# RWKV attention and SwiGLU on one core: two more units turned by VectorE, weight sums on VectorE, last store in halves

## The chip, the cores and the metric

The kernel runs on one core of a Trainium2 chip. The metric is device time in microseconds, the median over several executions; one more execution was profiled.

## What is computed

The reference is an RWKV attention block and a SwiGLU feed-forward block behind it, all in float32:

```python
# r, k, v: (4 batches, 8 heads, 768 positions, 48); w, u: (8, 48)
for t in range(S):
    cur = einsum('bhd,bhe->bhde', u[None] * kt, vt)
    y[:, :, t] = einsum('bhd,bhde->bhe', rt, state + cur)
    state = w[None, :, :, None] * state + einsum('bhd,bhe->bhde', kt, vt)
x = y.transpose(0, 2, 1, 3).reshape(3072, 384)
g = x @ w_gate                      # 384 x 1536
out = (g * sigmoid(g) * (x @ w_val)) @ w_out   # 1536 x 384
```

## The kernel before

The sequence is cut into chunks of 128 positions. A chunk of one batch with all its heads is a **unit**; there are 24 units, numbered chunk by chunk, so that unit i is chunk i // 4 of batch i % 4. For each unit:

- `load` and `load_v` bring k, r and v in through SyncE's DMA queue. From unit 4 on, k and r land in two alternating buffers (`k_ld`, `r_ld`).
- `scale` (GpSimd, L299 and L302) multiplies k and r by powers of the decay and writes them to `hats`, a tile that holds four k buffers (`khat`) and two r buffers (`rhat`). Which r buffer a unit takes is told by `rhat_of`: units below `BLOCKS` alternate, later ones go by pairs.
- `own_product` (GpSimd, L228 and L229) and `own_sum` (VectorE, L234) form the term of the current position. `load(i)` overwrites what the `own_product` of unit i - 2 reads, and so waits for it.
- k and r must be turned, so that the head's dimension lies on the partitions. Units below `BLOCKS` (12 before) use `turn`: eight transposes on TensorE into PSUM (L341) and two copies by ScalarE (L345). Units from `BLOCKS` on use `move_blocks` and `turn_blocks`: sixteen DMAs from SyncE's queue (L356) move the 32x32 blocks of `hats` to their turned places in two more buffers (`blocks`, one set only), and VectorE then turns each block in place with two instructions (L371).
- `scores` (TensorE L379, VectorE L384), `outputs` (TensorE L409, ScalarE L413) and `update` (TensorE L424, VectorE L436, GpSimd L437) give the attention's output x, and the state for the next chunk.

Two units make a group g of 256 rows for the feed-forward block. The groups 0 and 1 use `gate_value` (six matmuls into a PSUM bank of the tag gv, a sigmoid on ScalarE, L455 and L456 on VectorE). Later groups go in pairs through `four` and `w_sums` (L585 to L641), and all pairs go through `project` (L519 to L542), which needs fewer products than the plain form because it adds and subtracts quarters of the operands first. For that, `weight_sum` (L476, GpSimd before) makes four differences of quarters of `wo`, once; `h_sums` (L492 to L496, VectorE) makes those of the hidden layer. `project(g, 0)` takes PSUM banks of the tag gv, which has two buffers.

The weights come in as bits of another format and are rounded on the way (L173 to L216) by ScalarE, VectorE and GpSimd, up to about step 9. `EARLY` says at which points of the steps 4 to 11 a piece of rounding or, once that is done, a `weight_sum` ("R") and a piece of the feed-forward work ("F") is put in.

The order on every engine is the order of the code, as each engine works through its own queue. In step s of the main loop (s = 4 to 25) come: `own_sum(s)`, `scale(s + 1)`, `own_product(s + 1)`, `load_v(s + 1)`, `load(s + 3)`, then `turn(s)`, then `scores(s - 1)`, `turn_blocks(s)`, `move_blocks(s + 1)`, and, in steps before 12, `outputs(s - 2)` and `update(s - 2)` late in the step (from step 12 on right behind `scores`). The pieces of the feed-forward work stand between them.

Of the kernel before, what the change touches and what calls it, by code (L numbers as in the profile page):

```python
# [15 lines left out]
P = 128  # L16
# [6 lines left out]
def fast(  # L23
# [31 lines left out]
    N = B * NCH  # L55
    DM, DFF = moe_w_gate.shape
# [11 lines left out]
    dve, pool, act, pe, sp = nc.vector, nc.gpsimd, nc.scalar, nc.tensor, nc.sync  # L68
# [26 lines left out]
    khat, rhat = [hats[:, n] for n in (0, 2, 3, 5)], [hats[:, n] for n in (1, 4)]  # L95
# [4 lines left out]
    blocks = [hats[:, n].rearrange("p h x -> p (h x)") for n in (7, 6)]  # L100

    def rhat_of(i):
        return rhat[i % 2 if i < BLOCKS else i % 4 // 2]

    def raw(i):

# [4 lines left out]
    def load(i):  # L111
        c, b = divmod(i, B)
        rows = slice(P * c, P * (c + 1))
        for src, dst in zip((k, r), raw(i)):
            sp.dma_start(out=dst, in_=src[b, :, rows, :].rearrange("h t d -> t h d"))

    def load_v(i):
        c, b = divmod(i, B)
        rows = slice(P * c, P * (c + 1))
        for e in range(2):  # L120
            sp.dma_start(
                out=v_ld[i % 4][:, :, 64 * e : 64 * e + D],
                in_=v[b, :, rows, :].rearrange("(a e) t d -> e t a d", e=2)[e],
            )
# [3 lines left out]
    for f in range(FC // 2):  # L128
        for src, dst in ((moe_w_gate, wg), (moe_w_val, wv)):
            cols = slice(2 * P * f, 2 * P * (f + 1))  # L130
# [94 lines left out]
    def own_product(i):  # L225
        kl, rl = raw(i)
        rk = two.tile([P, H, D], FP32, name="rk", tag="rk")[:]
        pool.tensor_mul(rk, rl, kl)  # L228
        pool.tensor_mul(rk, rk, ub[:])  # L229
        rks[i] = rk  # L230

    def own_sum(i):
        dus[i] = three.tile([P, H], FP32, name="du", tag="du")
        dve.tensor_reduce(dus[i][:], rks.pop(i), axis=AX.X, op=ALU.add)  # L234
# [9 lines left out]
    for e in range(2):  # L244
# [3 lines left out]
        out=ub[:].rearrange("p h d -> p (h d)"),  # L248
        in_=bass.AP(tensor=u.tensor, offset=u.offset, ap=[[0, P], [1, H * D]]),
# [9 lines left out]
    def warm(n):  # L259
# [9 lines left out]
        out=mask[:], in_=mask[:], compare_op=ALU.is_gt, fill=0.0,  # L269
# [7 lines left out]
    for l in range(7):  # L277
        n = 1 << l
# [15 lines left out]
    def at(i, a):  # L294

        return HP - 1 - a if i >= BLOCKS and i % 2 == 0 else a

# [3 lines left out]
    def scale_r(i):  # L301
        pool.tensor_mul(rhat_of(i)[:, :, 0:D], raw(i)[1], rscale[:])  # L302
# [8 lines left out]
    def scale(i):  # L311
        scale_k(i)
        scale_r(i)
# [18 lines left out]
    def pair(t, a):  # L332
        return t[:, 2 * a : 2 * a + 2, :].rearrange("p e d -> p (e d)")

    def turn(i):
        kr = khat[i % 4], rhat_of(i)
        tps = [ps_a.tile([P, HP, P], FP32, name="tp", tag="a") for _ in kr]
        turned[i] = three.tile([P, HP, P], FP32, name="rT", tag="rT")
        for tp, t, dst, table in zip(tps, kr, (kT[i % 2], turned[i]), (pw[:, :, 1 : P + 1], pv)):
            for a in range(HP):  # L340
                pe.transpose(tp[:, a, :], pair(t, a), ident[:])  # L341
            if i < 4:
                dve.tensor_mul(dst[:], tp[:], table)
            else:
                act.copy(dst[:], tp[:])  # L345
# [27 lines left out]
    def scores(i):  # L373

        ps = [ps_a.tile([P, HP, P], FP32, name="s_ps", tag="a") for _ in range(2)]
        for a in range(HP):
            for e in range(2):
                rows = slice(64 * e, 64 * e + D)
                pe.matmul(  # L379
                    ps[e][:, a, :], kT[i % 2][rows, at(i, a), :], turned[i][rows, at(i, a), :],  # L380
                    start=True, stop=True, skip_group_check=True,
                )
        for e in range(2):
            dve.copy_predicated(  # L384
                At[i % 2][:].rearrange("p (a e) t -> p a e t", e=2)[:, :, e],
                mask[:].bitcast(INT32).unsqueeze(1).to_broadcast([P, HP, P]), ps[e][:],
            )
# [77 lines left out]
    FH, NH = FC // 2, DM // 2  # L465
# [5 lines left out]
    def weight_sum():  # L471

        n = len(summed)
        o = (wt[1][:], w12, wt[0][:], wt[2][:])[n]
        a, b = ((w22, w12), (w12, w11), (w22, w12), (w21, wt[0][:]))[n]
        pool.tensor_sub(o, a, b)  # L476
        summed.append(n)

    part_of = {}
# [1 line left out]
    def h_quarters(g):  # L481
        return [
            hT[g][:, FH * k : FH * (k + 1), P * j : P * (j + 1)] for j in range(2) for k in range(2)
        ]
# [13 lines left out]
    def project(g, n):  # L498

        h11, h12, h21, h22 = h_quarters(g)  # L500
        x = part_of.setdefault(g, {})
        if n == 0:
            one_bank = ps_f.tile([P, 2, 2 * P], FP32, name="o_f", tag="gv")[:, 0, 0:NH]
            if g % 2 == 0:
                x["a"] = ps_o.tile([P, 2 * P], FP32, name="o_a", tag="o")[:, 0:NH]
                x["b"] = one_bank
            else:
                x["a"] = one_bank
                x["b"] = ps_w.tile([P, 2 * P], FP32, name="o_b", tag="w_mag")[:, 0:NH]
            x["out"] = [two.tile([P, DM], FP32, name=n, tag=n) for n in ("o_sb1", "o_sb2")]  # L510
        lhs, rhs, acc = (
            (h11, w11, "a"), (h12, w21, "b"), (1, wt[0], "a"), (2, wt[1], "a"),
            (0, w12, "b"), (h22, wt[2], "a"), (3, w22, "b"),
        )[n]
        if isinstance(lhs, int):
            lhs = x["s"][lhs]
        ps = x[acc]
        for f in range(FH):
            pe.matmul(  # L519
                ps, lhs[:, f, :], rhs[:, f, :],  # L520
                start=(f == 0 and n in (0, 1, 4)), stop=(f == FH - 1), skip_group_check=True,
            )
        o1, o2 = x["out"]
        if n in (0, 2, 3):
            nm = {0: "p1", 2: "u2", 3: "u3"}[n]
            x[nm] = six.tile([P, 2 * P], FP32, name=nm, tag="part")[:, 0:NH]
            act.copy(x[nm], ps)
        elif n == 1:
            dve.tensor_add(o1[:, 0:NH], x["p1"], ps)
        elif n == 5:  # L530
            act.copy(o2[:, 0:NH], ps)
        elif n == 6:
            dve.tensor_add(o1[:, NH:DM], x["u2"], ps)  # L533
        if n in (3, 4):
            if "c22" in x:
                dve.tensor_add(o2[:, NH:DM], x["u3"], x["b"])
            x["c22"] = True
        if n >= 5:
            j = 6 - n
            c, b = divmod(2 * g + j, B)  # L540
            n0 = S * b + P * c
            act.dma_start(out=out[n0 : n0 + P, :], in_=x["out"][j][:])  # L542

# [155 lines left out]
    def gaps(s, n):  # L701

        if s not in EARLY:
            if n == 0:
                share[0] = min(-(-len(todo) // (4 - (s - 9) % 4)), 14)
            feed(share[0] // 5 + (n < share[0] % 5))
            return
        for what in EARLY[s][n]:
            if what == "R":
                if done["pool"] < NW:  # L710
                    round_weights()
                elif len(summed) < 4:
                    weight_sum()
            else:
                feed(1, 3)

    share = [0]
    BLOCKS = 12
    LATE = 12
    EARLY = {s: ("" if s < 7 else "R", "F", "R", "F", "RF") for s in range(5, 12)}  # L720
    EARLY[4] = ("R", "F", "", "F", "F")
# [82 lines left out]
    for s in range(4, N + 2):  # L804
        if 4 < s < N:
            own_sum(s)
        if s + 1 < N:
            scale(s + 1)
            own_product(s + 1)
            load_v(s + 1)  # L810
            if s + 3 < N:
                load(s + 3)
        if s < BLOCKS:
            turn(s)
        gaps(s, 0)
        if 4 <= s - 1 < N:
            while small:
                small.popleft()()
            scores(s - 1)
            if s >= LATE:  # L820
                outputs(s - 2)
                update(s - 2)
            gaps(s, 1)
        if BLOCKS <= s < N:
            turn_blocks(s)
        if BLOCKS <= s + 1 < N:
            move_blocks(s + 1)
        gaps(s, 2)
        if s - 2 >= 4 and (s < LATE or s > N):
            outputs(s - 2)  # L830
            update(s - 2)
        if s >= 5 and s % 2:
            queue((s - 3) // 2)
        if s < N:
            diagonal(s)
        if s - 2 >= 4:
            gaps(s, 3)
        gaps(s, 4)
        if s == 12:

            dve.tensor_tensor(bad[:], held[:], wcol[:], ALU.not_equal)
            dve.tensor_reduce(badc[:], bad[:], axis=AX.X, op=ALU.add)
            dve.memset(ones[:], 1.0)
            n_ps = ps_a.tile([P, HP, P], FP32, name="n_ps", tag="a")
            pe.matmul(n_ps[0:1, 0, 0:1], badc[:], ones[:], start=True, stop=True)
            act.copy(outside, n_ps[0:1, 0, 0:1])
# [417 lines left out]
```

## Time and profile before

| | us |
|---|---|
| median of 6 runs (625.54 to 627.76) | 626.11 |
| the profiled execution, its own time | 625.23 |
| span of its profile | 623.4 |
| TensorE busy in the span | 611.2 |
| VectorE / ScalarE / GpSimd busy | 357.6 / 238.8 / 296.8 |

Times in the profile run from the start of the span. A line of a timeline gives the start, the time from the start of the first to the end of the last instruction of the row, the engine (PE TensorE, PEld its weight loads, DVE VectorE, ACT ScalarE, POOL GpSimd, SP SyncE; a q behind it is the engine's queue, for DMA issues), the line, the operation, what it writes and reads, how many instructions, and in brackets the idle time ahead of it with what ended it. Busy time of an engine that others do not wait for costs nothing.

### The profile page before, as it was taken

Reading aid. Unit: us, or ns where it says so; the run is one execution under the profiler, and the core shown is the slowest. Engines: PE = TensorE matmul, PEld = TensorE weight load, DVE = VectorE, ACT = ScalarE, POOL = GpSimd, SP = SyncE. Lnnn points to the kernel's source line nnn. Section 1 sums busy time; section 2 is a strip of 40 time slices with the busy share of each in tenths; the row PEclk is TensorE's granted clock in tenths of the full one; section 3 lists DMA queues with packets and bytes.
Section 4 is the critical chain, followed back from the end, with each engine's and each line's share of the span. In section 5 each row is a group of like instructions: output and inputs, shape, how many; then the busy total and the mean of one; then the engine's idle time right before and its main releaser. Section 6 shows DMA issues by size and latency. Waiting matters only on the chain.

```text
span 623.4 us, 13014 instructions
## 1 busy us (share of the span) xinstructions
PE 611.2 (98%) x5040; PEld 551.4 (88%) x5040; DVE 357.6 (57%) x751; ACT 238.8 (38%) x647; POOL 296.8 (48%) x350
## 2 busy tenths in 40 slices
PE   8899999999999999999999999999999999999996
PEld 7688888899888899888899888899988899988896
DVE  5888897373566574466575455574354463355460
ACT  3368795312444412344331335422244321333310
POOL 4789789935556315364452636341334211443110
PEclk9999999999999999999999999999999999999999
DMA  7989873233232213323223311221000000000001
GB/s 179 221 218 249 257 249 64 51 63 83 56 60 34 39 16 77 64 42 46 45 34 68 78 17 31 32 41 38 26 1 2 2 0 26 26 1 2 1 2 56
DMA packets 138008, 40.47 MB, mean 65 GB/s; under 512 B 128592, under 2 KB 131792, under 8 KB 137936
## 3 DMA queue, kind: packets, MB, share of 16 engines
q1 hardware_dynamic: 134480, 34.82, 26.3%
q10 hardware_dynamic: 3456, 4.72, 2.1%
q8 instruction: 42, 0.69, 0.5%
q14 instruction: 30, 0.25, 0.1%
HBM read 28.51 MB, written 4.72 MB: 53 GB/s over the span
## 4 chain that ended last, share of the span: by engine, by line
PE 90%; POOL 2%; DMA 1%; ACT 1%; DVE 1%; issue 0%; SPq 0%; ACTq 0%; POOLq 0%
PE c_b L625 25%; PE c_a L625 21%; PE o_f L519 13%; PE o_a L519 8%; PE gv L448 7%; PE o_b L519 6%; PE y_ps L409 5%; PE s_ps L379 3%; PE u_ps L424 1%; DMA r_ld<-in_r_dram 1%; PE tp L341 1%; POOL wg L216 1%; POOL wv L216 1%; POOL rk L228 0%; POOL hats L299 0%
## 5 line engine op out<-in xcount | busy, mean ns | idle before, releaser
L609 POOL TENSOR_TENSOR hT<-hT,u 128x256 f32<-128x256 f32 x60 | 47.1, 785 | 148.3 <-DVE hT L608 121.2
L632 ACT COPY u<-c_a 128x256 f32<-128x256 f32 x120 | 44.5, 371 | 86.1 <-PE c_a L625 83.3
L625 PE MATMUL c_a<-t,wv 128*128 128x256 f32 x240 | 72.0, 382 | 0.1
L625 PE MATMUL c_b<-xT,wg 128*128 128x256 f32 x240 | 71.6, 380 | 0.0
L605 ACT ACTIVATE sg<-hT 128x256 f32<-128x256 f32 x120 | 50.0, 416 | 52.4 <-DVE hT L634 33.8
L320 ACT ACTIVATE At<-ident,du 128x128 f32<-128x128 f32 x176 | 62.1, 400 | 15.5 <-DVE o_sb L533 7.2
L625 PE MATMUL c_b<-xT,s 128*128 128x256 f32 x240 | 61.6, 379 | 0.0
L639 DVE TENSOR_TENSOR u<-u,c_b 128x256 f32<-128x256 f32 x60 | 25.1, 419 | 60.5 <-PE c_b L625 53.7
L625 PEld LDWEIGHTS c_b<-xT,s 128*128 128x128 f32 x240 | 45.2, 190 | 6.6
L625 PEld LDWEIGHTS c_a<-t,wv 128*128 128x128 f32 x240 | 44.9, 190 | 6.9 <-ACT u L632 1.2
L625 PEld LDWEIGHTS c_b<-xT,wg 128*128 128x128 f32 x240 | 45.3, 190 | 6.0
L634 DVE TENSOR_TENSOR hT<-p,c_b 128x256 f32<-128x256 f32 x60 | 25.2, 420 | 42.0 <-PE c_b L625 39.4
L585 POOL TENSOR_TENSOR s<-wv,wg 128x256 f32<-128x256 f32 x24 | 17.8, 741 | 65.5 <-PE o_f L519 50.8
L384 DVE COPY_PREDICATED At<-mask,s_ps 128x512 f32<-128x512 int32 x48 | 33.1, 744 | 21.8 <-PE s_ps L379 12.8
L302 POOL TENSOR_TENSOR hats<-r_ld,rscale 128x384 f32<-128x384 f32 x20 | 20.8, 1039 | 35.2 <-DMA hats<-hats 24.6
L448 PE MATMUL gv<-xT,wg 128*128 128x256 f32 x144 | 36.7, 391 | 0.6 <-ACT xT L413 0.6
L637 DVE TENSOR_TENSOR hT<-hT,c_a 128x256 f32<-128x256 f32 x60 | 25.3, 421 | 19.4 <-PE c_a L625 18.1
L641 DVE TENSOR_TENSOR hT<-u,c_b 128x256 f32<-128x256 f32 x60 | 25.2, 420 | 19.4 <-PE c_b L625 19.2
L409 PE MATMUL y_ps<-At,v_ld 128*32 128x128 f32 x768 | 34.9, 273 | 1.4 <-DVE At L384 1.4
L625 PE MATMUL c_b<-t,s 128*128 128x256 f32 x120 | 36.2, 383 | 0.0
L625 PE MATMUL c_b<-xT,wv 128*128 128x256 f32 x120 | 35.9, 381 | 0.0
L625 PE MATMUL c_a<-t,s 128*128 128x256 f32 x120 | 35.8, 380 | 0.0
(135 smaller groups left out, 1382.8 us busy)
## 6 DMA issues: line engine op xcount, KB each, us to landing
hats<-hats SPq DMA_DIRECT2D x192, 32.0 KB, 2.0
w_bits<-in_moe_w_gate_dram SPq DMA_DIRECT2D x6, 768.0 KB, 6.5
v_ld<-in_v_dram SPq DMA_DIRECT2D x48, 96.0 KB, 3.2
w_bits<-in_moe_w_val_dram SPq DMA_DIRECT2D x6, 768.0 KB, 6.1
w_bits<-in_moe_w_out_dram SPq DMA_DIRECT2D x6, 768.0 KB, 6.8
out_dram<-o_sb ACTq DMA_DIRECT2D x24, 192.0 KB, 1.9
k_ld<-in_k_dram SPq DMA_DIRECT2D x20, 192.0 KB, 3.1
r_ld<-in_r_dram SPq DMA_DIRECT2D x20, 192.0 KB, 3.9
```

The source lines that it names most:

```text
L320: lambda h=h: act.activation(At[i % 2][:, h, :], ident[:], AF.Identity, scale=du[:, h : h + 1])
L384: dve.copy_predicated(At[i % 2][:].rearrange("p (a e) t -> p a e t", e=2)[:, :, e], mask[:].bitcast(INT32).unsqueeze(1).to_broadcast([P, H ...
L409: pe.matmul(ps[32 * q : 32 * q + 32, cc, :], *x, start=start, stop=stop, skip_group_check=True,)
L448: pe.matmul(gv[:, o, :].rearrange("p (i t) -> p i t", i=2), wt[:, c, P * f : P * (f + 1)], xT[:, 2 * g % NX : 2 * g % NX + 2, c, :], start ...
L519: pe.matmul(ps, lhs[:, f, :], rhs[:, f, :], start=(f == 0 and n in (0, 1, 4)), stop=(f == FH - 1), skip_group_check=True,)
L605: act.activation(x[what, f][:], h[j], AF.Sigmoid)
L609: pool.tensor_mul(h[1], h[1], x.pop(("u3", f))[:])
L625: pe.matmul(ps.rearrange("p (i t) -> p i t", i=2), lhs, rhs, start=first, stop=what not in ("p2", "p5", "p4", "p3"), skip_group_check=True,)
L632: act.copy(x[nm, f][:], ps)
L634: dve.tensor_add(h[0], x.pop(("p1", f))[:], ps)
L637: dve.tensor_mul(h[0], h[0], ps)
L641: dve.tensor_add(h[1], x.pop(("u2", f))[:], ps)
```

## The change

`BLOCKS` becomes 10, so the units 10 and 11 are no longer turned by TensorE and ScalarE but moved by DMAs and turned by VectorE. The r buffers go by pairs from unit 8 on: 8 and 9 share one, 10 and 11 the other. Since unit 9 then overwrites what `turn(8)` reads, `turn(s)` is put ahead of `scale(s + 1)`. The four weight sums go to VectorE, at the same points of the order. For the very last output the left half of the row block is stored as soon as it is ready, and the last store takes the right half alone.

```diff
     def rhat_of(i):
-        return rhat[i % 2 if i < BLOCKS else i % 4 // 2]
+        return rhat[i % 2 if i < 8 else i % 4 // 2]
...
     def weight_sum():
...
-        pool.tensor_sub(o, a, b)
+        dve.tensor_sub(o, a, b)
...
     def project(g, n):
...
-        if n >= 5:
-            j = 6 - n
+        def store(j, cols):
             c, b = divmod(2 * g + j, B)
             n0 = S * b + P * c
-            act.dma_start(out=out[n0 : n0 + P, :], in_=x["out"][j][:])
+            act.dma_start(out=out[n0 : n0 + P, cols], in_=x["out"][j][:, cols])
+
+        ends = g == N // 2 - 1
+        if n == 1 and ends:
+            store(0, slice(0, NH))
+        elif n >= 5:
+            store(6 - n, slice(NH if n == 6 and ends else 0, DM))
...
-    BLOCKS = 12
+    BLOCKS = 10
...
     for s in range(4, N + 2):
         if 4 < s < N:
             own_sum(s)
+        if s < BLOCKS:
+            turn(s)
         if s + 1 < N:
             scale(s + 1)
             own_product(s + 1)
             load_v(s + 1)
             if s + 3 < N:
                 load(s + 3)
-        if s < BLOCKS:
-            turn(s)
         gaps(s, 0)
```

## The prediction

> **What bounds the kernel now.** First the page's shares and the chain that ended last, to see which engine sets the end:
>
> ```profile
> PE 611.2 (98%) x5040; PEld 551.4 (88%) x5040; DVE 357.6 (57%) x751; ACT 238.8 (38%) x647; POOL 296.8 (48%) x350
> PE 90%; POOL 2%; DMA 1%; ACT 1%; DVE 1%; issue 0%; SPq 0%; ACTq 0%; POOLq 0%
> ```
>
> TensorE is busy for 611.2 of 623.4 us. The merged chain has other engines only before 57.8 us; from there to 618 us it is TensorE alone, and the waits of TensorE after 57 us hold one entry, 0.3 us long. So from 57.8 us on, TensorE work taken out is time won, and any new wait of TensorE is lost in full. Every edit lies in that part. The question is only whether TensorE ever has to wait. For that I read the timelines of the single engines around the change (start, duration, engine, line, then the wait in brackets). TensorE:
>
> ```profile
> 101.49 1.04 PE L341 MATMUL tp<-ident,hats 128*128 128x128 f32 x8
> 102.46 1.16 PE L379 MATMUL s_ps<-rT,kT 48*128 48x128 f32 x16
> ...
> 123.20 2.11 PE L519 MATMUL o_a<-wo,hT 128*128 128x192 f32 x12
> 125.15 4.06 PE L519 MATMUL o_f<-wo,hT 128*128 128x192 f32 x24
> ```
>
> The x8 are unit 10's transposes; unit 11's lie at 113.64. The x24 at 125.15 begin with the first six passes of the second projection of the pair (g = 1, n = 0). They write the PSUM bank (tag gv) that the last gate_value before them used, so they must wait for VectorE's L456 on that bank. VectorE:
>
> ```profile
> 123.81 0.42 DVE L455 TENSOR_TENSOR sg<-sg,gv 128x256 f32<-128x256 f32 x1 [2.41 <-ACT sg L454]
> 124.27 0.42 DVE L456 TENSOR_TENSOR hT<-sg,gv 128x256 f32<-128x256 f32 x1
> ...
> 141.08 0.71 DVE L371 STREAM_TRANSPOSE kT<-hats 128x512 f32<-128x512 f32 x1
> 141.71 0.67 DVE L371 STREAM_TRANSPOSE rT<-hats 128x512 f32<-128x512 f32 x1
> 142.31 0.38 DVE L567 TENSOR_TENSOR t<-xT 128x256 f32<-128x256 f32 x1
> ```
>
> L456 ends at 124.69, 0.46 us before TensorE needs the bank. That is all the room there is. SyncE's queue, and GpSimd at the first unit that is moved today (12):
>
> ```profile
> 94.33 0.37 SPq L115 DMA_DIRECT2D k_ld<-in_k_dram  x1
> 94.75 0.57 SPq L115 DMA_DIRECT2D r_ld<-in_r_dram  x1
> ...
> 119.39 0.57 SPq L115 DMA_DIRECT2D r_ld<-in_r_dram  x1
> 120.02 10.95 SPq L356 DMA_DIRECT2D hats<-hats  x16
> 131.07 1.09 SPq L121 DMA_DIRECT2D v_ld<-in_v_dram  x2
> 134.77 0.37 SPq L115 DMA_DIRECT2D k_ld<-in_k_dram  x1
> 135.19 0.57 SPq L115 DMA_DIRECT2D r_ld<-in_r_dram  x1
> ```
>
> ```profile
> 132.76 1.02 POOL L302 TENSOR_TENSOR hats<-r_ld,rscale 128x384 f32<-128x384 f32 x1 [8.02 <-DMA hats<-hats]
> 133.73 1.01 POOL L228 TENSOR_TENSOR rk<-r_ld,k_ld 128x384 f32<-128x384 f32 x1
> ```
>
> One unit's move is sixteen small DMAs that hold SyncE for 10.95 us (0.65 us apart). GpSimd's next scale_r, which overwrites the moved buffer, starts 1.79 us after the last issue ends. Today's moves start 22 us and more apart (the second at 142.41); units 10 and 11 are turned 12.15 us apart (101.49 and 113.64).
>
> **Transposes off TensorE: the gain.** From the start of the eight transposes to the start of the scores is 0.97 us; two units give 1.94 us (the chain's 0.87 each would give 1.74). [...] ScalarE loses four copies (0.57 and 0.59 us), which lay beside TensorE: no time by itself.
>
> **The moves added to SyncE: the cost.** After the change SyncE's order is: load(12), move 10, load_v(11), load(13), move 11, load_v(12), load(14), move 12. I follow it with the rows above.
> - load(12) waits for unit 10's rk as now and ends at 94.75 + 0.57 = 95.32. Move 10 starts at 95.38, and at 10.95 us it ends at 106.33.
> - Unit 11 shares its r buffer (rhat 1) with unit 10, so scale_r(11), now at 103.97, waits until 106.33 + 1.79 = 108.12. Its rk starts 0.97 us later (132.76 to 133.73), at 109.09.
> - load(13) overwrites what rk reads. It goes out 1.04 us after rk's start (133.73 to 134.77), at 110.13, and ends at 111.12.
> - Move 11 stands behind it and behind VectorE's turn_blocks(10), which has its data at 108.12 and is through at 109.35. So it starts at 111.18, ends at 122.13 and has landed at 123.92.
> - VectorE waits there for turn_blocks(11). Behind it in its queue are unit 9's two Z additions (0.77 us from start to the next) and the last L455 and L456 (0.88 us). So 123.92 + 1.23 (141.08 to 142.31) + 0.77 + 0.88 = 126.80.
>
> TensorE, 1.94 us ahead, wants that bank at 125.15 - 1.94 = 123.21. It gets it at 126.80, with 0.05 us for the handover (ScalarE's sigmoid ends at 123.79, VectorE starts at 123.81) at 126.85. The stall is 3.64 us, and the sum 3.64 - 1.94 = +1.70 us. In other words the bank's release moves from 124.69 to 126.80, and the 0.46 us of room and the whole gain are used up by it. How much the transposes cost on TensorE drops out of the end: a larger gain only makes a longer stall.
>
> Bounds: other moves in this trace hold SyncE for 10.41 to 11.29 us, and the wait after them is 1.46 us at its shortest (a move from 165.81 to 176.22, scale_r at 177.68) and 1.80 at its longest. Both occur twice in the chain. The short ends take 2 x (0.54 + 0.33) = 1.74 us off, so -0.04; the long ones add 2 x 0.34 + 0.02 = 0.70, so +2.40. I take 10.95 and 1.79, since move 12 stands directly behind a load, as 10 and 11 will; the 10.4 us ones all start with nothing in front.
>
> What comes after the stall is hidden. The h sums that the third projection step needs end near 129.3, and TensorE gets there at 126.85 + 3.9 = 130.75. Move 12 runs from 125.2 to 136.1 and lands at 137.9, while VectorE wants it at 141.08 + 1.7. Unit 13's scale_r slips from 132.76 to 137.9 and its rk to about 141, read by L234 at 151.50. load_v(11) slips by 10 us, load_v(12) by 14; their units' outputs come in steps 13 and 14. If one of these covers failed, the miss would be added one for one.
>
> **The weight sums.** GpSimd loses 4 x 2.63 = 10.5 us, and has 4.1 us of it taken by the wait for move 10. On VectorE no row has 1152 elements: 256 take 0.42 us and 768 take 0.95, which extends to 1.35, so 5.4 us in all. The far bound is GpSimd's own 2.63. A VectorE sum beside GpSimd work took 1.37 instead of 0.95 (L493 at 594.75), which is between. VectorE is busy for 5.08 of 12.15 us in one of the stages and 6.17 of 12.16 in the other. By its own queue it reaches turn_blocks(11) at about 118.5, and has to wait until 123.92 anyway. So 5.4 us are hidden, and even at 2.63 each (5.1 us more) it would arrive at 123.6. Cost: nothing, and below nothing is excluded, because GpSimd's sums kept nobody waiting.
>
> **The small edits.** turn(s) ahead of scale(s + 1) matters for unit 9 alone: scale_r(9) starts at 79.55 and unit 8's transposes end at 78.24, so 1.3 us cover it. The last output: ScalarE's last two stores are issued from 616.38 to 618.71 and the span ends at 623.4. A DMA of 0.8 KB lands in 1.9 us by the page, and so does one of 192 KB, so 96 KB in place of 192 saves between 0 and 0.1 us. I take 0. The added early store waits at about 600.8 in ScalarE's queue for VectorE, and the copy behind it runs at 604.39: hidden.
>
> **Sum.** The profiled execution took 625.23 us (623.4 and 1.83 around it), 0.88 less than the median, so it becomes 626.93, and the median 626.11 + 1.70 = 627.8.
>
> **The rivals.**
> - No difference: the two moves run at their short ends and the bank comes free about when TensorE reaches it today, -0.04 us: 626.1. For it: nine of twelve moves hold SyncE for under 10.9 us. Against it: the move that most resembles the new ones does not.
> - Faster: TensorE never waits for the bank and the 1.94 us are won: 624.2. That needs a chain 3.6 us shorter. Were issues 0.609 us apart (their median duration) instead of 0.65, two moves would give 2.4 and the short landings 0.7, so most of it. Against: start to start is 0.65 in every move I looked at. A waiting order in VectorE's queue that I have misplaced would also do it.
> - Slower by more: the stall costs TensorE its clock as well. At the start of the trace TensorE issues 7 matmuls in each of the microseconds up to 8, and later 9 transposes in 0.86, though the clock column reads 1.00; so after idleness it was slow for over 5 us. [...] Against: the longest later gap in the trace is 1.19 us, and nothing slow follows it; nothing shows a gap of 3.6. [...]
>
> **Numbers.** Forecast 0.63 (its own range +0.7 to +2.5 us, 626.8 to 628.6), no difference 0.13, faster 0.13, slower by more 0.11. A measurement of this kernel can tell about 0.2%, 1.25 us, from no change. Some 0.10 of the forecast lies under +1.25, so slower 0.64, same 0.21, faster 0.15. The range takes in both near cases and reaches toward the gain and the clock loss: 624.7 to 629.5.
>
> **What would show it.** In the profile after: VectorE's transposes of units 10 and 11 (L371) near 108 and 124 us, with VectorE idle for some 5 us before the second and a DMA as releaser; SyncE's moves at 95.4 and 111.2; GpSimd's scale_r waiting about 4 us; TensorE idle once, before o_f, for some 3.6 us; the weight sums at 1.35 to 1.8 us each with no one waiting. I am wrong if TensorE shows no gap near 123 us, if the gap sits elsewhere, or if the second move starts well before 111.

## The result, and the profile after

The changed kernel took 628.18 us (median of 22 runs, 625.70 to 631.83) against 626.48 us for the kernel before on the same chip (46 runs, 625.37 to 628.20). The ratio is 1.003 with a 95% interval of 1.0022 to 1.0038, so 1.4 to 2.4 us slower. Its profiled execution took 626.95 us, with a span of 625.1 (before: 625.23 and 623.4).

The page of the changed kernel, its busy shares, the chain that ended last, and the DMA issues of the moves:

```profile
PE 609.7 (98%) x5024; PEld 549.1 (88%) x5024; DVE 367.1 (59%) x759; ACT 237.0 (38%) x643; POOL 290.5 (46%) x346
PE 81%; SPq 5%; DMA 5%; DVE 2%; POOL 2%; ACT 2%; issue 1%; ACTq 0%; DVEq 0%; POOLq 0%
hats<-hats SPq DMA_DIRECT2D x224, 32.0 KB, 2.0
```

TensorE's sixteen transposes are gone (5040 to 5024 instructions, 1.5 us less busy), the moves are 224 small DMAs instead of 192, and SyncE's queue and the DMAs, hardly on the chain before, now hold 10% of it. What TensorE waits for after 57 us (engine, line, releaser, total us, times, longest):

```profile
PE y_ps L409 <- ACT kT L345: 1.4, 1, 1.4
PE o_f L519 <- DVE hT L456: 0.8, 1, 0.8
PE o_a L519 <- DVE hs L493: 0.6, 1, 0.6
PE c_a L630 <- ACT p L637: 0.3, 1, 0.3
```

The first entry lies at 59 us, ahead of the first added move (96 us) and the first weight sum (105 us). Of the edits only the new order of turn and scale comes before it, and e1_rest, which has that order too, has 0.3 us there, as later profiles of the same kernel have 0.3 and 0.4: it is scatter of the start. The second and third are new. The four engines around them, TensorE first:

```profile
122.89 2.11 PE L519 MATMUL o_a<-wo,hT 128*128 128x192 f32 x12
124.84 2.11 PE L519 MATMUL o_f<-wo,hT 128*128 128x192 f32 x12
127.74 2.19 PE L519 MATMUL o_f<-wo,hT 128*128 128x192 f32 x12 [0.78 <-DVE hT L456]
130.48 2.19 PE L519 MATMUL o_a<-wt,hs 128*128 128x192 f32 x12 [0.55 <-DVE hs L493]
```

A row's x12 is one projection step: six matmuls, each of which the trace shows as two passes. The x24 of before is torn in two. Its first half, project(1, 0), runs at 124.84 with L456 still to come; the second half, project(0, 1), waits for L456. (The order is told by who takes the results: ScalarE's copy at L527 reads the first at 126.99, VectorE's L529 the second at 131.99.) SyncE:

```profile
95.03 0.37 SPq L115 DMA_DIRECT2D k_ld<-in_k_dram  x1
95.45 0.57 SPq L115 DMA_DIRECT2D r_ld<-in_r_dram  x1
96.08 11.20 SPq L356 DMA_DIRECT2D hats<-hats  x16
...
111.04 0.37 SPq L115 DMA_DIRECT2D k_ld<-in_k_dram  x1
111.46 0.58 SPq L115 DMA_DIRECT2D r_ld<-in_r_dram  x1
112.13 11.23 SPq L356 DMA_DIRECT2D hats<-hats  x16
```

GpSimd, where scale_r(11) waits for the first move, and rk behind it holds load(13):

```profile
109.06 1.00 POOL L302 TENSOR_TENSOR hats<-r_ld,rscale 128x384 f32<-128x384 f32 x1 [3.90 <-DMA hats<-hats]
110.03 0.99 POOL L228 TENSOR_TENSOR rk<-r_ld,k_ld 128x384 f32<-128x384 f32 x1
```

VectorE:

```profile
110.29 1.94 DVE L476 TENSOR_TENSOR wo<-wo 128x1152 f32<-128x1152 f32 x1
...
120.04 0.42 DVE L456 TENSOR_TENSOR hT<-sg,gv 128x256 f32<-128x256 f32 x1
124.76 0.71 DVE L371 STREAM_TRANSPOSE kT<-hats 128x512 f32<-128x512 f32 x1 [4.29 <-DMA hats<-hats]
...
127.17 0.42 DVE L456 TENSOR_TENSOR hT<-sg,gv 128x256 f32<-128x256 f32 x1
127.51 0.54 DVE L234 TENSOR_REDUCE du<-rk 128x8 f32<-128x384 f32 x1
127.97 1.37 DVE L492 TENSOR_TENSOR hs<-hT 128x768 f32<-128x768 f32 x1
129.38 0.96 DVE L493 TENSOR_TENSOR hs<-hs,hT 128x768 f32<-128x768 f32 x1
```

VectorE idles for 4.29 us at turn_blocks(11) with the last L456 and the h sums (L492, L493) queued behind it. Those two are what TensorE then waits for.

### The profile page after: what moved, and what is told of

Same layout as the page of the kernel before. It is cut to its first block, busy times and chain, and to the rows that moved or that the text cites. A ratio compares the mean times of both kernels' runs of the same rounds, so it can differ in the third digit from the quotient of the medians.

```text
span 625.1 us, 13021 instructions
## 1 busy us (share of the span) xinstructions
PE 609.7 (98%) x5024; PEld 549.1 (88%) x5024; DVE 367.1 (59%) x759; ACT 237.0 (38%) x643; POOL 290.5 (46%) x346
## 4 chain that ended last, share of the span: by engine, by line
PE 81%; SPq 5%; DMA 5%; DVE 2%; POOL 2%; ACT 2%; issue 1%; ACTq 0%; DVEq 0%; POOLq 0%
PE c_b L630 23%; PE c_a L630 19%; PE o_f L519 12%; PE o_a L519 7%; PE o_b L519 6%; PE y_ps L409 5%; SPq L356 5%; PE gv L448 4%; PE s_ps L379 3%; DMA hats<-in_r_dram 2%; DMA w_bits<-in_moe_w_val_dram 1%; DMA hats<-hats 1%; DMA ub<-in_u_dram 1%; PE u_ps L424 1%; ACT At L320 0%
## 5 line engine op out<-in xcount | busy, mean ns | idle before, releaser
L630 PE MATMUL c_a<-xT,wg 128*128 128x256 f32 x120 | 35.8, 380 | 0.0
```

The costliest lines, as they stand in the source:

```text
L630: pe.matmul(ps.rearrange("p (i t) -> p i t", i=2), lhs, rhs, start=first, stop=what not in ("p2", "p5", "p4", "p3"), skip_group_check=True,)
```

## The experiments

Each kernel is the changed one with one edit, measured beside the kernel before on the same chip. There were three chips, so kernels of different groups are compared by their differences to before. The theory: the added moves are late, VectorE waits for them at turn_blocks(11), and what is queued behind that wait holds TensorE. The rivals: the weight sums on VectorE are the cause, or the other small edits are.

**All edits but the moves (e1_rest).**

```diff
-    BLOCKS = 10
+    BLOCKS = 12
```

> The change without its moves: BLOCKS = 12 again, with the weight sums on VectorE, the turn ahead of the scale and the halved last store kept. Theory A (the two added moves hold SyncE so long that VectorE's wait for unit 11 delays TensorE): nothing of that is left, TensorE never waits after 60 us, and only the shorter tail shows, 0 to 0.4 us faster than before. Rival B (the weight sums take 1.6 to 1.9 us each on VectorE and push its queue late): the loss of about 1.9 us stays or part of it, TensorE waits near 123 us. Rival C (the turn ahead of the scale makes the first 60 us slower, TensorE 1.4 us behind at 60 us as in the profile after): the loss stays, and the TensorE row at 57 to 60 us is late again.

625.42 against 625.52 us, ratio 1.0 (0.9991 to 1.0009). TensorE's waits after 57 us in its profile:

```profile
PE c_a L630 <- ACT p L637: 0.3, 1, 0.3
PE y_ps L409 <- ACT kT L345: 0.3, 1, 0.3
```

Neither new wait is there. The weight sums on VectorE (1.42 to 1.71 us each here), the new order of turn and scale and the split store are worth nothing measurable, alone. The loss needs the moves.

**One of the two units (e2_eleven).** `BLOCKS = 11`: unit 10 stays on TensorE, unit 11 is moved.

> Only unit 11 is moved (BLOCKS = 11), unit 10 is turned by TensorE again. Theory A: without move 10 ahead of it, move 11 starts near 107 and lands near 120, as VectorE arrives there; no stall of TensorE near 125, one set of transposes saved: 0.97 us and the tail's 0.3, so 1.0 to 1.4 us faster than before. Rival B: same sums on VectorE, so still no faster than before, 0 to 1 us slower. Rival C: 0 to 0.5 us slower.

625.02 against 625.52, ratio 0.9996 (0.9987 to 1.0005): 0.5 us less by the medians, which can't be told from nothing, where more was expected. SyncE and TensorE in its profile:

```profile
107.40 11.32 SPq L356 DMA_DIRECT2D hats<-hats  x16
```

```profile
124.06 4.06 PE L519 MATMUL o_f<-wo,hT 128*128 128x192 f32 x24
```

With no move 10 in front, move 11 starts 4.7 us earlier and the x24 is whole. So it is the two moves in a row that make the wait.

**The wait put behind the work that others need (e3_late, repeated as e12_late).** In step 11 alone, turn_blocks and move_blocks come after the last piece of feed-forward work:

```diff
+        def blocks_step():
+            if BLOCKS <= s < N: turn_blocks(s)
+            if BLOCKS <= s + 1 < N: move_blocks(s + 1)
-        if BLOCKS <= s < N:
-            turn_blocks(s)
-        if BLOCKS <= s + 1 < N:
-            move_blocks(s + 1)
+        if s != 11:
+            blocks_step()
...
         gaps(s, 4)
+        if s == 11:
+            blocks_step()
```

> The changed kernel with turn_blocks(11), and move 12 behind it, put at the end of step 11, behind the last L455 and L456 in VectorE's queue; SyncE's order and the data's times are the same. Theory A: the bank comes free at about 123 instead of 127.6, the h sums end about 1.3 us earlier, TensorE waits less than 0.5 us in all; about 1.3 to 1.8 us faster than the changed kernel, so 0 to 0.4 us slower than before or up to 0.5 faster. Rivals B and C: no difference to the changed kernel, 1.9 us slower than before.

> The order with unit 11's turn at the end of step 11, beside the changed kernel on one chip. Theory A: 1.5 to 2.8 us faster than the changed kernel, 0.8 to 1.4 us faster than before; no wait of TensorE above 0.5 us near 125 us.

624.45 against 625.52, ratio 0.9983 (0.9974 to 0.9992); repeated, 624.59 against 625.62, 0.9982 (0.9973 to 0.9991). That is 1.0 us faster than the kernel before, and 2.2 us less than the changed kernel measured beside the repeat (e11_after). VectorE and TensorE in the profile of e3_late:

```profile
122.82 0.42 DVE L456 TENSOR_TENSOR hT<-sg,gv 128x256 f32<-128x256 f32 x1
124.40 0.71 DVE L371 STREAM_TRANSPOSE kT<-hats 128x512 f32<-128x512 f32 x1 [1.16 <-DMA hats<-hats]
```

```profile
123.70 4.06 PE L519 MATMUL o_f<-wo,hT 128*128 128x192 f32 x24
128.14 2.19 PE L519 MATMUL o_a<-wt,hs 128*128 128x192 f32 x12 [0.38 <-DVE hs L493]
```

The data come no sooner (the transposes start at 124.40, in the changed kernel at 124.76), but L456 is now ahead of the wait and the x24 is whole. Move 12, which the edit takes along, starts at 125.73 us (126.09 in the changed kernel). The moves by themselves do no harm: the place of the wait in VectorE's queue does. What stays is the h sums' wait, 0.38 us here and 0.92 in the repeat, and with it the gain falls short of the two units' 1.75 us.

**The move put ahead of load(13) (e4_swap), and both together (e5_swap_late).** At s = 10, `load(s + 3)` is issued right after `move_blocks(s + 1)`:

```diff
-            if s + 3 < N:
+            if s + 3 < N and s != 10:
                 load(s + 3)
...
+        if s == 10:
+            load(s + 3)
```

> The changed kernel with load(13) put behind move 11 in SyncE's queue, so that the move does not wait for GpSimd's rk of unit 11. Theory A: move 11 starts near 110.3 instead of 112.1 and lands 1.8 us earlier, VectorE and the h sums are through 1.8 us earlier, and TensorE's two waits of 1.7 us in all go away: 1.4 to 2.0 us faster than the changed kernel, about as fast as before or up to 0.6 us faster. Rivals B and C: no difference to the changed kernel.

> Both shifts at once: turn_blocks(11) at the end of step 11 and load(13) behind move 11. Theory A: with the late order alone one wait was left, 0.38 us before the third projection step, for the h sums, which stand behind unit 11's turn in VectorE's queue; with the data 1 us earlier it goes. No wait of TensorE near 125 us; 0.2 to 0.5 us faster than the late order alone, so 1.2 to 1.6 us faster than before. If the moves' own scatter (10.4 to 11.9 us in SyncE's queue) is what is left, no difference to the late order.

e4_swap: 625.08 against 625.52, ratio 0.9992 (0.9983 to 1.0001). SyncE's moves in its profile:

```profile
95.86 11.94 SPq L356 DMA_DIRECT2D hats<-hats  x16
...
110.97 11.67 SPq L356 DMA_DIRECT2D hats<-hats  x16
```

The second move starts 1.2 us sooner than in the changed kernel, but both took longer, and 1.2 and 0.6 us of waiting remain. Its median is 0.4 us below that of before, where the changed kernel's lie above, in the direction that the theory says; the interval just includes no difference to before. e5_swap_late: 624.23 against 625.37, 0.9989 (0.9978 to 1.0), the x24 whole, and no measurable gain over e3_late. In its profile the h sums' wait is gone too (TensorE begins the third step at 127.49, 3.97 us after the start of the x24), but the medians show nothing of that.

**The changed kernel again (e6_after, e11_after), and its weight sums back on GpSimd (e7_sums_pool).** For e7, in weight_sum:

```diff
-        dve.tensor_sub(o, a, b)
+        pool.tensor_sub(o, a, b)
```

> The changed kernel again, beside its variants on one chip. In its first profile TensorE was already 1.4 us late at 60 us, by a wait that no other profile shows, which hid a part of the stall. Theory A: in a profile without that lateness, the two waits of TensorE near 125 us are longer, 2.2 to 3.2 us in all, and the time is 1.4 to 2.4 us above before. Rival C (the early lateness belongs to the change): it is there again.

> The changed kernel with the weight sums back on GpSimd. Theory A: they stand behind rk of unit 11 in GpSimd's queue, so move 11 is not touched, and VectorE has to wait for its data all the same: the loss against before stays at 1.4 to 2.4 us, within 0.5 us of the changed kernel, unless the sums now come too late for the third projection step (then up to 3 us more). Rival B: VectorE's queue is 5.4 to 7 us lighter, the loss is gone, 0 to 1 us faster than before.

> The changed kernel a third time, because the first measurement (0.3% slower) and the second (0.16%) differ. Theory A with D: the loss moves with the length of the two moves in SyncE's queue and with whether the wait is long enough for the clock to drop; 0.7 to 1.9 us slower than before, a profile with 22.3 us or more for the two moves shows the longer waits. If the changed kernel is really no slower, under 0.5 us.

e6_after: 626.08 against 625.37, ratio 1.0016 (1.0007 to 1.0026). e11_after: 626.83 against 625.62, 1.0025 (1.0011 to 1.004). e7_sums_pool: 626.00 against 625.37, 1.0018 (1.0 to 1.0036). With the sums off VectorE the loss stays at 0.6 us by the medians (its interval just reaches no difference), and in e1_rest the sums alone cost nothing, so they are not its cause. TensorE in the profile of e6_after:

```profile
121.44 2.11 PE L519 MATMUL o_a<-wo,hT 128*128 128x192 f32 x12
...
126.45 2.19 PE L519 MATMUL o_f<-wo,hT 128*128 128x192 f32 x12 [0.94 <-DVE hT L456]
129.19 2.19 PE L519 MATMUL o_a<-wt,hs 128*128 128x192 f32 x12 [0.55 <-DVE hs L493]
```

This profile has the start of before (unit 9's transposes at 89.34 and 89.35 us), so it sets out the sum: TensorE is at the projection at 121.44 instead of 123.20, 1.76 us ahead, and has lost that again at the third step, 129.19 against 129.05. The waits are smaller than I had expected. TensorE in the profile of e7_sums_pool, then its windows (from:to and length, busy us of PE, PEld, DVE, ACT, POOL with the number of instructions, granted clock, DMA share, GB/s):

```profile
123.70 2.11 PE L519 MATMUL o_f<-wo,hT 128*128 128x192 f32 x12
127.80 3.77 PE L519 MATMUL o_f<-wo,hT 128*128 128x192 f32 x12 [1.99 <-DVE hT L456]
```

```profile
128.00:130.00 2.00, 2.00 (x8) 2.00 (x8) 1.97 (x3) 0.00 (x0) 1.92 (x2) 0.56 0.40 63
130.00:132.00 2.00, 2.00 (x9) 2.00 (x9) 2.00 (x3) 0.00 (x0) 0.14 (x1) 0.59 0.37 49
```

In this execution the two moves took 11.70 and 11.54 us and the wait was 1.99 us. After it twelve passes took 3.77 us instead of 2.19, at a granted clock of 0.56 to 0.59 for 4 us. That is the prediction's dearer rival, in one execution of a kernel whose median shows nothing of it.

**The wait dosed (e8_dose), and TensorE kept at work in it (e9_dose_warm, e10_after_warm).** Four small DMAs into a spare tile go ahead of move 11. In the second kernel TensorE also has fifteen matmuls without use in the wait (x30 in the row), ahead of project(0, 1). The third is the changed kernel without the dose and with four of these, warm(4).

```diff
+        for m in range(4 if i == 11 else 0):
+            sp.dma_start(out=spare[32 * m : 32 * m + 32], in_=...)
...
             elif (j, p) == (0, 6) and g + 2 < N // 2:
                 x_sums(g + 2)
+            if (g, j, p) == (0, 0, 1):
+                warm(15)
```

> The changed kernel with four more small DMAs (same sources as the first four of move 11, 12 of 32 columns, into a spare tile that nobody reads) ahead of move 11 in SyncE's queue. Theory A: each holds SyncE for about 0.65 us, move 11 lands 2.6 us later, and TensorE's wait grows by as much: 2.2 to 3.0 us slower than the changed kernel, 3.8 to 5.2 us slower than before. Rivals B and C: no difference to the changed kernel.

> The kernel with four more DMAs, and in the gap that they open on TensorE, fifteen matmuls of the identity (0.22 us each, 3.3 us in all) ahead of the second projection's waiting passes; nobody reads what they write. Theory D (a wait of 2 us or more drops TensorE's granted clock to about half for the next 4 us, which is the 1.6 us that the wait alone does not explain): the bank comes free at the same time, 129.5, but the twelve passes behind it take 2.1 to 2.2 us and not 3.9, the granted clock stays at 1.00: 1.3 to 1.8 us faster than without them, about 3.6 to 4.2 us slower than before. [...]

> The changed kernel with four such matmuls (0.9 us) in the same place. Theory D: where the wait is short, as in its second profile (0.94 us), nothing changes; where it is near 2 us, the clock no longer drops. So the upper runs (628 to 630 us) become rare, and the median lies 0 to 0.6 us under the changed kernel's, 0.4 to 1.0 us above before. If the spread has another cause, no difference in the spread.

e8_dose: 630.47 against 625.37, ratio 1.0088 (1.0075 to 1.0101). SyncE and TensorE in its profile:

```profile
110.76 2.70 SPq L355 DMA_DIRECT2D spare<-hats  x4
113.56 11.19 SPq L366 DMA_DIRECT2D hats<-hats  x16
```

```profile
129.51 3.87 PE L529 MATMUL o_f<-wo,hT 128*128 128x192 f32 x12 [4.06 <-DVE hT L466]
```

Against e6_after it lost 4.4 us by the medians. The dose accounts for 2.8 of that (110.76 to 113.56). The twelve passes behind the wait are 3.87 us long instead of 2.19, of which about 1.0 counts: TensorE begins the third step at 133.21, 3.70 us after their start, where e6_after, with its second wait, needed 2.74 (126.45 to 129.19). That second wait is gone here: the profile lists none for the h sums. e9_dose_warm has the same dose and took 629.26 against 625.41, 1.0063 (1.0051 to 1.0076), 1.2 us less than e8_dose (the intervals just touch); TensorE in its profile:

```profile
125.67 3.51 PE L264 MATMUL warm<-ident 128*128 128x128 f32 x30
129.95 2.19 PE L529 MATMUL o_f<-wo,hT 128*128 128x192 f32 x12 [0.77 <-DVE hT L466]
```

The passes start no earlier, but take 2.19 us again, at a granted clock of 1.00 from 130 to 132 us (e8_dose: 0.50); the wait for the h sums is back (0.56 us). So idleness cost TensorE its clock here, and time with it: 1.2 us by the medians. e10_after_warm was a miss: 626.46 against 625.41, 1.0014 (1.0005 to 1.0023), no less than the changed kernel. Its profiled execution is the slowest of its twelve, 628.34 us, and its trace tells most of why. TensorE, then one of its windows:

```profile
25.04 0.66 PE L341 MATMUL tp<-ident,hats 128*128 128x128 f32 x4 [1.48 <-DMA hats<-in_k_dram]
...
123.98 2.11 PE L519 MATMUL o_a<-wo,hT 128*128 128x192 f32 x12
...
129.68 2.19 PE L519 MATMUL o_f<-wo,hT 128*128 128x192 f32 x12 [0.75 <-DVE hT L456]
```

```profile
28.00:32.00 4.00, 4.00 (x89) 3.66 (x87) 2.61 (x8) 0.00 (x0) 0.96 (x1) 0.50 0.98 222
```

Here the granted clock fell to 0.50 in the start, behind a wait of 1.48 us for a load, and not at the wait in question, behind which it is 1.00 and the passes take 2.19 us: TensorE reaches the projection at 123.98, 2.54 us later than in e6_after. So time lost in an execution of these kernels need not be lost at 125 us.

## Why the prediction was right, and where its steps were not

The direction and the cause stand: the moves are late on SyncE, VectorE waits for the second, and TensorE waits for what stands behind (shown by e1, e2, e3 and e8). The size, +1.70 us, lies in the measured 1.4 to 2.4, but by terms that were wrong and made up for each other: that it is so near is luck, and the two repeats gave +0.7 and +1.2.

- **Which passes wait: the step that failed.** I gave the bank to the first six matmuls of the x24, with 0.46 us of room and a stall of 3.64. It is the next six, project(0, 1), that wait for it. Before, these began at 125.15 + 1.95 = 127.10, so the room was 127.10 - 124.69 = 2.41 us. In the profile of the changed kernel the wait is 127.74 - (124.84 + 1.95) = 0.95 us, in e6_after 126.45 - (123.39 + 1.95) = 1.11.
- **The h sums were not hidden.** Two rows, L492 and L493, end at 130.3 instead of the 129.3 that I had, since the L456 ahead of them ended 0.79 us later than forecast and L492 took 1.37 us (0.94 in e3_late), and TensorE, less late than forecast, came for them sooner. Their wait adds 130.48 - (127.74 + 1.95) = 0.79 us.
- **The gain** was 1.76 us (e6_after), the chain's 0.87 per unit, and not the 1.94 that I took.
- **The moves** took 11.20 and 11.23 us instead of 10.95. Over the kernels with both moves unchanged the first took 11.0 to 11.8, and the "longest" row of before, 11.29, was no bound. The queue's order and what released what were as forecast: transposes at 124.76 (forecast 123.92), wait 4.29 (about 5), bank at 127.59 (126.80), scale_r's wait 3.90 (about 4).
- **The weight sums** took 1.57 to 1.94 us, partly above my 1.8, and hid in VectorE's wait, as forecast. e7 confirms it.
- **The tail** gained 0.3 us in this profile (4.74 instead of 5.07 from the last output addition to the end), which e1_rest's median doesn't show.
- **The clock rival** (0.11) was seen in e7_sums_pool's profile, behind a wait of 1.99 us: a granted clock of 0.56 to 0.59 for 4 us. No run shows the 1.7 us for a clock loss that lie between the forecast, 627.8, and the range's upper end, 629.5. What the runs showed in its place: twelve passes took 3.77 us instead of 2.19 in that profile, and 3.87 in e8_dose's, of which about 1.0 counted.

By the profiles the terms sum to 0.95 + 0.79 - 1.76, about nothing, in the changed kernel, and to 1.11 + 0.79 - 1.76 = +0.14 in e6_after. The rest of the difference between these executions and that of before stands elsewhere. TensorE's last projection step begins 2.03 us behind before's in the changed kernel (617.86 against 615.83): 1.43 of a late start, and 0.6 that come in behind the third step, 0.34 of them in the c_a row of its waits. The tail gives 0.3 back, which leaves the 1.72 us between the two executions. In e6_after the last step is 0.80 behind, in e1_rest, which has no added moves, 0.96 (0.75 of it from behind 131.30 us), so this later part need not be the moves' doing. Whether it is scatter of these runs, or the one profile of before lies low (625.23 against a median of 626.11), is open.

The medians say +0.7 to +1.7. The profiled executions thus lie at the low end of what the medians show, and a share of the loss is in executions that I have no profile of. Dearer ones exist: e7's profile, and two runs of e11_after at 629.90 and 630.27 us with mean clocks of 0.995 and 0.993, where its other runs end at 627.34. That a longer wait and then a slower clock make the rest is argued from these, not shown, and a mean clock does not say where it was lost: e10_after_warm's profiled execution has 0.995 too, from the start, and two runs of e2_eleven have 0.995 at 624.91 and 625.02 us. Also open is why sixteen like DMAs hold SyncE for anything from 10.4 to 11.9 us. In the changed kernel's chain single issues take 1.23 us where most take 0.61. Of the 191 moves in the profiles here the 100 under 10.5 us have no issue above 0.7 us, and all but one of those from 11.0 us on have an issue above 1 us; what makes an issue long is not shown.

## What to carry to other kernels

VectorE's wait for a DMA (4.29 us at turn_blocks(11)) held up the L456 queued behind it, and TensorE with that for 0.95 us: put an instruction that waits for a DMA behind the work that others wait for. Moving one such pair in a single step turned a loss of 0.7 to 1.7 us into a gain of 1.0. Before a stall is priced, find the very instruction that takes the freed buffer; naming its neighbour was worth 1.95 us here. And allow for the scatter of the moves on SyncE's queue: like moves took 10.4 to 11.9 us here, and two stood ahead of a room of 2.41 us.

## What was not expected of the hardware

TensorE's clock fell after a wait of 1.99 us (e7_sums_pool, 0.56 to 0.59 for 4 us) and after 4.06 (e8_dose, 0.50 from 130 to 132 us), and in the shown rows not after 0.78 or 0.94, where it stayed at 1.00 and twelve passes took 2.19 us. The length of the wait alone does not decide it: in e10_after_warm the clock fell in the start (0.50 from 28 to 32 us) behind one of 1.48 us and, 1 us on, one of 0.51, and in e8_dose it stayed at 1.00 behind one of 1.82 us at the same place:

```profile
24.68 0.66 PE L342 MATMUL tp<-ident,hats 128*128 128x128 f32 x4 [1.82 <-DMA hats<-in_k_dram]
```

Some float32 additions and products of VectorE and GpSimd that overlap in time took longer than their like elsewhere: an L229 2.01 us in the changed kernel and 1.00 in the kernel before, an L492 1.37 us and 0.95 in e1_rest. GpSimd in the profile of the changed kernel:

```profile
110.03 0.99 POOL L228 TENSOR_TENSOR rk<-r_ld,k_ld 128x384 f32<-128x384 f32 x1
111.09 2.01 POOL L229 TENSOR_TENSOR rk<-rk,ub 128x384 f32<-128x384 f32 x1
...
127.53 1.00 POOL L299 TENSOR_TENSOR hats<-k_ld,kscale 128x384 f32<-128x384 f32 x1
```

L476 on VectorE takes 1.94 us (three of the four L476 in e2_eleven take 1.35). It starts at 110.29, while L228 runs until 111.02, and ends at 112.23, which is 1.21 us after that; L229 ends at 113.10, 0.87 us after L476. L492, from 127.97 to 129.34, lies behind L299 in the same way (0.81 us from 128.53). In these three pairs the later row thus ends 0.81 to 1.21 us after the earlier one, each a little less than its own length elsewhere; the rows do not show why. The prediction had the stretch of the h sums in a row that it named for another purpose (L493, 1.37 us at 594.75), and did not apply it to them.
